# Two blocks of the first layer: plain first contractions, and second ones together by seven products of halves

## The chip, the cores and the metric

The kernel runs on one core of one Trainium2 chip. TensorE (PE in the profile) multiplies matrices, VectorE (DVE) and ScalarE (ACT) work elementwise, GpSimd (POOL) does a few small copies, and SyncE (SP) issues most DMAs. The metric is device time in microseconds (us): 1556.63 as the median of three runs (1556.58 to 1556.65).

## The reference

Linear attention without a softmax, an RMS norm per head, and two MLPs on the 4608 resulting tokens of width 512 (d_ff is 2048):

```python
kv = np.einsum('bhsd,bhse->bhde', k, v)        # q, k, v: (8, 8, 576, 64)
out = np.einsum('bhsd,bhde->bhse', q, kv)
rms = np.sqrt(np.mean(out * out, axis=-1, keepdims=True) + 1e-06)
x = (out / rms * g_norm)                       # then to (4608, 512)
# layer 1
h = x @ w_in                                   # 512 -> 2048
g = np.where(h >= 1, h, np.where(h <= -1, 0.0, (h + 1) ** 2 / 4))
x = g @ w_out                                  # 2048 -> 512
# layer 2
r = np.maximum(x @ w_in2, 0.0); out = (r * r) @ w_out2
```

Everything is float32.

## The kernel before

**Precision.** A float32 operand is split into a high part (a cast, L216) and a low part (the rest, a DVE subtraction, L229), and a product is three matmuls: high by high, high by low, low by high (`mm3`, L237; `mm_group` prints as L877). All counts of matmuls below contain this factor of three; one matmul is 128 x 128 weights against 512 columns.

**Blocks.** The tokens are cut into nine blocks of 512: block b (0 to 7) is the first 512 tokens of batch b, block 8 the eight remainders of 64. Layer 1 runs first over blocks 0 to 6 in the *plain* way: per block 16 steps f, each with 12 matmuls of the first contraction into a PSUM bank (`h_stage`, names `ph1_b_f`), the activation (relu on ACT L704, square on ACT L223, minimum and maximum on DVE L706), the split (`g_stage`: cast L216, rest L229), and, LAG = 2 steps later, 12 matmuls of the second contraction into four accumulators (`out_stage`, names `acc1_b_c`). `ph` has two PSUM buffers, the accumulators four banks.

Layer 1's blocks 7 and 8 and all pairs of layer 2 (`PAIRS`) are done two blocks at a time by *seven products of halves* instead of eight: `in_phase` forms sums of quarters of x, multiplies (336 matmuls, names `ph`), and combines on DVE; the activation follows; `out_phase` does the same with g (336 matmuls, names `po`). The sums of weight quarters are prepared earlier (`prep_load`, `prep_narrow`, `prep_sums`, `prep_split`), stored to DRAM, and loaded when wanted (`load_w2`, 512 KB each, on SP). A plain pair of blocks has 768 matmuls, a pair by seven products 672. The last block of layer 2 runs through the same phases with half the columns.

**Attention beside it.** While the plain blocks run, the attention of the next batches is worked in between. A batch has four *items*, one for each two heads (`hp`). An item is kv (`kv_stage`, once for two items), the transposes and splits of q (`t_stage`), q times kv (`o_stage`), and the norm (`r_stage`): row sums of squares on PE (`pr`, L600), Ln and Exp on ACT (L601, L603), a square on ACT (L223), then on DVE a Newton step for the two column halves (L518) and two products (L521, L522), at last the split of x (cast L216 on ACT, rest L229 on DVE). Its result `x1_b_hp` is the input of block b.

**What sets the order.** `hook(s, f)` puts a job into half-step s (two to a plain step, 32 to a block); before, item j of batch b starts at half-step 32(b - 1) + 7j, and its norm is six half-steps later. The sums of weights are spread from half-step 36 on over 164. Each engine executes its instructions in program order and waits there for what they need. `Ring` hands out tiles of SBUF again after their last use.

Of the kernel before, what the change touches and what calls it, by code (L numbers as in the profile page):

```python
# [76 lines left out]
def linear_attention_rms_two_mlps(  # L77
# [42 lines left out]
    xp = ctx.enter_context(tc.tile_pool(name="xp", bufs=2 * KD))  # L120
# [11 lines left out]
    PLAIN = B - 1  # L132
    PAIRS = [(2, 0), (2, 2), (1, PLAIN), (2, 4), (2, 6)]
# [332 lines left out]
    def kv_stage(b, *hps):  # L466
        ps = bank(b, f"pkv_{b}_{hps[0]}")
        for n, hp in enumerate(hps):
# [10 lines left out]
        for n, hp in enumerate(hps):  # L479
# [149 lines left out]

    def begin(b):  # L630
        if b < LAST_B:
            new_x(1, b)
# [17 lines left out]
    def attention(b, base, every, order):  # L650

        slots = []
        for j, hp in enumerate(order):
            s = base + every * j
            turn.setdefault((b, hp), len(turn))
            if b == 1:
                slots += [(max(0, s - 7), load_kv, b, hp), (s, kv_stage, b, hp)]
            elif j % 2 == 0:
                two = order[j : j + 2]
                turn[b, two[1]] = len(turn)  # L660
                slots += [(max(0, s - 7), load_kv, b, i) for i in two]
                slots.append((s, kv_stage, b, *two))
# [6 lines left out]
            if j == 0:  # L669
# [4 lines left out]
        if b < LAST_B:  # L674
            slots.append((2 * NF * b, store_xrem, b))
# [10 lines left out]
    def h_stage(L, b, f):  # L686
        pool, tag = (ps_h, "h")
        if (L, b) == (1, 0) and 2 <= f < WAVE:
            pool, tag = (ps_a, f"acc{f - 2}")
# [11 lines left out]
        u = ep.tile([P, TB], F32, tag="e", name=f"u{L}_{b}_{f}")  # L701
# [8 lines left out]
        gs[L, b, f] = u  # L710
# [70 lines left out]
    for L in [L for L, _ in PAIRS] + [2]:  # L781
        w_order += [(L, 0, q, p) for q in range(NQ) for p in PRODUCTS]
# [108 lines left out]
    def in_phase(n):  # L891
# [244 lines left out]
    for i, t in enumerate((7, 9, 11, 13, 15, 21, 23)):  # L1136
        hook(last + t, load_w2)
# [53 lines left out]
    for t in range(N1):  # L1191
        h_stage(*step(t))
# [15 lines left out]
        pay()  # L1208
# [79 lines left out]
```

## Time and profile before

| | us |
|---|---|
| median of three runs | 1556.63 |
| span of the profiled execution | 1555.3 |
| around that span (their difference) | 1.3 |
| PE busy | 1546.2 |
| DVE busy | 1133.4 |
| ACT busy | 973.7 |

The span runs from the first to the last instruction of one profiled execution; a run's time has about 1.3 us more. PE is busy 99% of the span. Matmuls are pipelined, so the time that one costs is not its own duration but the distance to the next; the chain of waits shows it, as us for so many matmuls.

### The profile page before, as it was taken

To read this page: it belongs to the slowest core of one execution; us is meant where nothing else is said; L and a number is where in the kernel's file an instruction comes from. 1 tells how busy PE (TensorE), PEld (TensorE's weight loads), DVE (VectorE), ACT (ScalarE), POOL (GpSimd) and SP (SyncE) were. 2 spreads that over 40 slices of the span, in tenths; PEclk is the share of its full clock that TensorE was granted. 3 is DMA by queue.
4 is the path that set the end of the run, shared out by engine and by line. 5 is a ranking of instruction groups with operands and counts; after the bars stand their busy time and mean duration, and the time that the engine had idled before them with its cause. 6 is when DMAs were issued, how large, how long until landed. Compare 5 with 4: busy or idle time off the path is not lost.

```text
span 1555.3 us, 22355 instructions
## 1 busy us (share of the span) xinstructions
PE 1546.2 (99%) x7729; PEld 1283.6 (83%) x7729; DVE 1133.4 (73%) x2000; ACT 973.7 (63%) x1833; POOL 20.4 (1%) x38
## 2 busy tenths in 40 slices
PE   9999999999999999999999999999999999999999
PEld 5787888888888888888888888888888888888898
DVE  6986886877877776754587558778965596568666
ACT  5977766767666676665565466456646663565374
POOL 0000000000000000000000000000000000000000
PEclk9999999999999999999999999999999999999999
DMA  9666899996878967935676877696876676877796
GB/s 290 194 217 187 274 315 277 309 314 196 275 246 243 281 207 228 295 99 169 196 245 192 224 219 245 194 250 191 258 228 204 203 239 197 242 248 223 214 389 250
DMA packets 327520, 368.23 MB, mean 237 GB/s; under 512 B 196976, under 2 KB 222576, under 8 KB 327408
## 3 DMA queue, kind: packets, MB, share of 16 engines
q1 hardware_dynamic: 295360, 308.60, 66.9%
q10 hardware_dynamic: 32048, 58.20, 9.9%
q8 instruction: 61, 1.00, 0.3%
q14 instruction: 51, 0.42, 0.1%
HBM read 282.59 MB, written 84.15 MB: 236 GB/s over the span
## 4 chain that ended last, share of the span: by engine, by line
PE 97%; ACT 1%; DVE 1%; DMA 1%; issue 0%; DVEq 0%; ACTq 0%
PE po L877 27%; PE ph L877 27%; PE acc L237 19%; PE ph L237 18%; PE po L237 1%; PE pkv L478 1%; PE pr L600 1%; PE pwarm L1150 1%; DMA wf<-wsd 1%; ACT raw L267 0%; ACT w L216 0%; PE pr L533 0%; ACT u L704 0%; DVE t L518 0%; DVE w L184 0%; PE po L510 0%
## 5 line engine op out<-in xcount | busy, mean ns | idle before, releaser
L877 PE MATMUL ph<-x,ws 128*128 128x512 f32 (+1 forms) x2016 | 422.4, 371 | 0.0
L877 PEld LDWEIGHTS ph<-x,ws 128*128 128x128 f32 x2016 | 355.9, 188 | 65.5
L877 PE MATMUL po<-t,ws 128*128 128x512 f32 x1680 | 381.6, 389 | 0.0
L877 PEld LDWEIGHTS po<-t,ws 128*128 128x128 f32 x1680 | 315.4, 188 | 65.4
L237 PE MATMUL ph<-x,w 128*128 128x512 f32 x1344 | 329.3, 392 | 1.3 <-ACT w L216 0.6
L237 PEld LDWEIGHTS ph<-x,w 128*128 128x128 f32 x1344 | 248.8, 188 | 54.0 <-ACT w L216 1.4
L806 DVE TENSOR_TENSOR t<-g,t 128x512 fp32r<-128x512 f32 (+1 forms) x288 | 183.2, 641 | 91.2 <-ACT t L216 84.2
L216 ACT CAST t<-g 128x512 fp32r<-128x512 f32 (+1 forms) x288 | 165.7, 585 | 97.2 <-DVE t L806 50.4
L237 PE MATMUL acc<-gs,w 128*128 128x512 f32 x696 | 173.0, 392 | 1.5 <-DVE u L706 1.5
L237 PE MATMUL acc<-gs,wt 128*128 128x512 f32 x648 | 157.9, 391 | 0.0
L237 PEld LDWEIGHTS acc<-gs,w 128*128 128x128 f32 x696 | 128.6, 188 | 27.8 <-DVE u L706 2.0
L934 DVE TENSOR_TENSOR h<-ph,e 128x512 f32<-128x512 f32 (+1 forms) x144 | 92.7, 645 | 67.4 <-PE ph L877 59.9
L237 PEld LDWEIGHTS acc<-gs,wt 128*128 128x128 f32 x648 | 120.1, 188 | 24.3
L704 ACT ACTIVATE u<-ph,halfb 128x512 f32<-128x512 f32 x112 | 77.3, 690 | 88.7 <-PE ph L237 86.3
L706 DVE SCALAR_TENSOR_TENSOR u<-u,ph 128x512 f32<-128x512 f32 x112 | 76.3, 681 | 54.2 <-ACT u L223 53.8
L941 ACT ACTIVATE h<-h 128x512 f32<-128x512 f32 (+1 forms) x120 | 70.3, 586 | 61.8 <-DVE h L934 57.1
L927 DVE TENSOR_TENSOR e<-ph,e 128x512 f32<-128x512 f32 (+1 forms) x96 | 60.9, 643 | 48.4 <-PE ph L877 47.4
L216 ACT CAST gs<-u 128x512 fp32r<-128x512 f32 x112 | 69.7, 622 | 38.4 <-DVE u L706 35.8
L229 DVE TENSOR_TENSOR gs<-u,gs 128x512 fp32r<-128x512 f32 x112 | 76.8, 686 | 21.7 <-ACT gs L216 21.2
L216 ACT CAST x<-xr 128x512 fp32r<-128x512 f32 (+1 forms) x84 | 49.0, 586 | 40.5 <-DVE xr L857 19.4
L942 ACT ACTIVATE g<-h 128x512 f32<-128x512 f32 (+1 forms) x120 | 70.7, 589 | 3.2
L223 ACT ACTIVATE u<-u 128x512 f32<-128x512 f32 x112 | 70.8, 632 | 1.5 <-ACT u L704 0.6
(134 smaller groups left out, 1531.8 us busy)
## 6 DMA issues: line engine op xcount, KB each, us to landing
ws<-wsd SPq DMA_DIRECT2D x336, 512.0 KB, 4.4
wsd<-s ACTq DMA_DIRECT2D x96, 512.0 KB, 4.9
wt<-wsd SPq DMA_DIRECT2D x54, 512.0 KB, 5.6
raw<-in_moe_w_in_dram SPq DMA_DIRECT2D x32, 512.0 KB, 6.0
raw<-in_moe_w_out_dram SPq DMA_DIRECT2D x32, 512.0 KB, 6.4
xr<-x1d SPq DMA_DIRECT2D x36, 256.0 KB, 4.9
out_dram<-ov SPq DMA_DIRECT2D x142, 64.0 KB, 3.7
wsd<-w SPq DMA_DIRECT2D x17, 512.0 KB, 5.0
```

The source lines that it names most:

```text
L216: return e.copy(dst, src)
L223: e.activation(dst, src, AF.Square)
L229: lo = engine(op + "_lo", phase).tensor_tensor(t[:, 1, :], src, t[:, 0, :].bitcast(F32), ALU.subtract)
L237: nc.tensor.matmul(dst, wt(a), xt(c), start=first and n == 0, stop=last and n == 2)
L704: nc.scalar.activation(u, ps, AF.Relu, bias=halfb, scale=0.5)
L706: nc.vector.scalar_tensor_tensor(u, u, 1.0, ps, op0=ALU.min, op1=ALU.max)
L806: engine2(op + "_lo").tensor_tensor(t[:, 1, :], src, t[:, 0, :].bitcast(F32), ALU.subtract)
L877: nc.tensor.matmul(ps, wt(a), xt(c), start=first and n == 0 and i == 0, stop=last and n == len(lhs) - 1 and i == 2, skip_group_check=True,)
L927: nc.vector.tensor_tensor(e[i, p], bank, e[i, 1], ALU.add)
L934: nc.vector.tensor_tensor(h, bank, add, ALU.add)
L941: nc.scalar.activation(u, h, AF.Relu)
L942: nc.scalar.activation(g, u, AF.Square)
```

## The change

PLAIN goes from 7 to 5 and PAIRS gains (1, 5). Blocks 5 and 6 of layer 1 run 16 plain steps each for the first contraction only, without `out_stage` between them (half-steps from FULL = 160 on are then one step of 12 matmuls each; the banks of the accumulators serve as further buffers of `ph`). The activation writes into tiles that stay whole (`whole_g`), and there is no `g_stage`. `whole_sums` (two DVE subtractions for each of eight k) forms the first sums in the last eight steps, and then `out_phase(0)` does the second contraction of both blocks by seven products. `in_phase(0)`, which was interleaved with the end of the plain part, is gone; the jobs that prepare x for the next pair move into `out_phase(0)`.

Attention from block 2 on starts at the half-steps STARTS, mostly 6 instead of 7 apart, with batch 7's items laid between those of batches 4 to 6 and after them; the sums of weights are spread over 149 half-steps instead of 164. Rings and tags of SBUF tiles change accordingly.

```diff
-    PLAIN = B - 1
-    PAIRS = [(2, 0), (2, 2), (1, PLAIN), (2, 4), (2, 6)]
+    PLAIN = 5
+    PAIRS = [(1, PLAIN), (2, 0), (2, 2), (1, B - 1), (2, 4), (2, 6)]
...
+    STARTS = (32, 39, 46, 53, 60, 66, 72, 78, 84, 90, 96, 102, 109, 115, 121, 127, 133, 140)
+    STARTS += (146, 152, 158, 164, 169, 175)
+    SPREAD = 149
...
     def h_stage(L, b, f):
...
+        if (b > PLAIN or (b == PLAIN and f >= 4)) and f % 3 < 2:
+            pool, tag = (ps_a, f"acc{f % 3 + f // 3 % 2 * 2}")
...
-        u = ep.tile([P, TB], F32, tag="e", name=f"u{L}_{b}_{f}")
+        if b >= PLAIN:
+            u = whole_g(f % NH, b - PLAIN)[:, f // NH, :]
+        else:
+            u = ep.tile([P, TB], F32, tag="e", name=f"u{L}_{b}_{f}")
...
+    def whole_g(k, m):
+        tiles = g_whole.setdefault(k, [])
+        if len(tiles) == m:
+            tiles.append(whole_ring.tile([P, 2, TB], F32, f"g0_{k}_{m}"))
+        return tiles[m]
...
+    whole_ring = Ring(
+        *((wp, f"w1_{i}") for i in range(10)),
+        *((xp, f"x{KD + i}") for i in range(KD)),
+        *((wp, f"w0_{i}") for i in range(2)),
+    )
...
+    def sums_in(n, k):
+        a, b, d = g2[k][0][:, 0, :], g2[k][0][:, 1, :], g2[k][1][:, 1, :]
+        t1[k] = t1_ring.tile([P, TB], F32, f"t1_{n}_{k}")[:, : width(n)]
+        engine2("t_sum").tensor_tensor(t1[k], b, a, ALU.subtract)
+        engine2("t_sum").tensor_tensor(b, d, b, ALU.subtract)
+
+    def whole_sums(k):
+        g2[k] = [Quarters(g_whole[k], j) for j in range(2)]
+        sums_in(0, k)
...
-    blocks = [(1, b) for b in range(PLAIN)]
+    blocks = [(1, b) for b in range(PLAIN + 2)]
+    FULL = 2 * NF * PLAIN
...
-        hooks.setdefault((s // 2, s % 2), []).append((f, a))
+        place = (s // 2, s % 2) if s < FULL else (PLAIN * NF + s - FULL, 0)
+        hooks.setdefault(place, []).append((f, a))
...
-    for b in range(1, B):
-        jobs += attention(b, 2 * NF * (b - 1), 7, range(NP))
+    jobs += attention((0, 7, 14, 21), [(1, hp) for hp in range(NP)])
+    order = []
+    for b in range(2, LAST_B):
+        order += [(LAST_B, b - 4)] * (b >= 4) + [(b, hp) for hp in range(NP)]
+    order.append((LAST_B, NP - 1))
+    jobs += attention(STARTS, order)
...
-        which, i = j % 2, j // 2
-        s0 = 2 * NF + 4 + (j * 164) // 16
+        which, i = 1 - j % 2, j // 2
+        s0 = 2 * NF + 4 + (j * SPREAD) // 16
...
-    last = 2 * (PLAIN - 1) * NF
-    first_x = x2_jobs(0, Ring(*[(st, "st")] * 7))
-    when = [2, 3, 3, 4, 5, 6, 7, 8, 7, 9, 9, 10, 11, 12, 13, 14]
-    for t, f in zip(when, first_x):
-        hook(last + 2 * t + 1, f)
+    for i in range(NH):
+        hook(FULL + NF + NH + i, whole_sums, i)
...
     for t in range(N1):
+        plain = t < PLAIN * NF
         h_stage(*step(t))
...
-        if not WAVE // 2 <= t < WAVE:
+        if plain and not WAVE // 2 <= t < WAVE:
             g_stage(*step(t))
-        if t >= WAVE:
+        if WAVE <= t < PLAIN * NF + LAG:
             out_stage(*step(t - LAG))
...
     for n in range(NS + 1):
-        step_in = in_phase(n)
+        step_in = in_phase(n) if n else ()
         for i, _ in enumerate(step_in):
             pay(True)
-            if n == 0 and i < LAG:
-                out_stage(*step(N1 - LAG + i))
```

**PE, start of block 6.** Names: `ph1_6_f` is the first contraction of block 6, `x1_6_c` its input (c = 3 is the last item of batch 6), `pr_6_3` the row sums of that item's norm, in two halves; `x3` stands for three matmuls. Before:

```order
L237 MATMUL acc1_5_0_5628<-gs1_5_13_6310,wt5_13_6283 128x512 x3
L237 MATMUL acc1_5_1_5629<-gs1_5_13_6310,wt5_13_6283 128x512 x3
L237 MATMUL acc1_5_2_5630<-gs1_5_13_6310,wt5_13_6283 128x512 x3
L237 MATMUL acc1_5_3_5631<-gs1_5_13_6310,wt5_13_6283 128x512 x3
L237 MATMUL ph1_6_0_6434<-x1_6_0_5665,w1_0_0_300 128x512 x3
L237 MATMUL ph1_6_0_6434<-x1_6_1_5666,w1_0_0_300 128x512 x3
L237 MATMUL ph1_6_0_6434<-x1_6_2_5667,w1_0_0_300 128x512 x3
L237 MATMUL ph1_6_0_6434<-x1_6_3_5668,w1_0_0_300 128x512 x3
L478 MATMUL pkv_7_0_6452<-v_7_0_6269,k_7_0_6266 64x64 x8
```

After (the same place in the work):

```order
L603 MATMUL pr_6_3_1_6376<-s2lo_6_3_6329,ones_121 128x288
L240 MATMUL ph1_6_1_6427<-x1_6_0_5748,w1_0_1_366 128x512
L240 MATMUL ph1_6_1_6427<-x1_6_1_5749,w1_0_1_366 128x512 x3
L240 MATMUL ph1_6_1_6427<-x1_6_2_5750,w1_0_1_366 128x512 x3
L240 MATMUL ph1_6_4_6518<-x1_6_2_5750,w1_0_4_487 128x512 x2
L240 MATMUL ph1_6_5_6538<-x1_6_0_5748,w1_0_5_508 128x512 x3
L240 MATMUL ph1_6_5_6538<-x1_6_1_5749,w1_0_5_508 128x512 x3
L240 MATMUL ph1_6_5_6538<-x1_6_2_5750,w1_0_5_508 128x512
L240 MATMUL ph1_6_3_6482<-x1_6_0_5748,w1_0_3_464 128x512 x3
L240 MATMUL ph1_6_3_6482<-x1_6_1_5749,w1_0_3_464 128x512 x3
L240 MATMUL ph1_6_3_6482<-x1_6_2_5750,w1_0_3_464 128x512 x3
L240 MATMUL ph1_6_5_6538<-x1_6_2_5750,w1_0_5_508 128x512 x2
```

The next five rows are products with `x1_6_3`. In the changed kernel the norm of the last item of batch 6 ends with the first row, and the products of `x1_6_0` to `x1_6_2` are drawn ahead of those of `x1_6_3`; before, all of x1_6 was there, and products of block 5's second contraction stood ahead.

**PE, end of the plain part.** `t0_p_k` are the operands of `out_phase(0)` in product p, `ws` sums of weights. Before:

```order
L237 MATMUL ph1_6_15_7338<-x1_6_3_5668,w1_0_15_1150 128x512 x3
L237 MATMUL acc1_6_0_6619<-gs1_6_13_7262,wt6_13_7239 128x512 x3
L237 MATMUL acc1_6_1_6620<-gs1_6_13_7262,wt6_13_7239 128x512 x3
L237 MATMUL acc1_6_2_6621<-gs1_6_13_7262,wt6_13_7239 128x512 x3
L237 MATMUL acc1_6_3_6622<-gs1_6_13_7262,wt6_13_7239 128x512 x3
L877 MATMUL ph0_1_0_7372<-x2_0_1_0_6731,ws2_0_0_1_6739 128x512 x3
L877 MATMUL ph0_1_0_7372<-x2_0_1_1_7076,ws2_0_0_1_6739 128x512 x3
L877 MATMUL ph0_1_1_7383<-x2_0_1_0_6731,ws2_0_0_1_6739 128x512 x3
L877 MATMUL ph0_1_1_7383<-x2_0_1_1_7076,ws2_0_0_1_6739 128x512 x3
```

After:

```order
L240 MATMUL ph1_6_15_6778<-x1_6_0_5748,w1_0_15_1150 128x512 x3
L240 MATMUL ph1_6_15_6778<-x1_6_1_5749,w1_0_15_1150 128x512 x3
L240 MATMUL ph1_6_15_6778<-x1_6_2_5750,w1_0_15_1150 128x512 x3
L240 MATMUL ph1_6_15_6778<-x1_6_3_5751,w1_0_15_1150 128x512 x3
L914 MATMUL po0_1_0_6817<-t0_1_0_6805,ws1_1_0_1_6576 128x512
L914 MATMUL po0_1_1_6818<-t0_1_0_6805,ws1_1_0_1_6576 128x512
L914 MATMUL po0_1_0_6817<-t0_1_0_6805,ws1_1_0_1_6576 128x512 x2
L914 MATMUL po0_1_1_6818<-t0_1_0_6805,ws1_1_0_1_6576 128x512 x2
L914 MATMUL po0_1_0_6817<-t0_1_1_6808,ws1_1_0_1_6576 128x512
L914 MATMUL po0_1_1_6818<-t0_1_1_6808,ws1_1_0_1_6576 128x512
```

Before, products of `in_phase` alternate with the second contraction of the last steps. In the changed kernel the first product of `out_phase(0)` stands right behind the last first contraction.

**DVE, the same place.** `g0_k_m` are the whole activations, L715 their minimum and maximum, L988 and L987 the sums, L843 the low part of an operand. After:

```order
L715 SCALAR_TENSOR_TENSOR g0_5_1_6551<-g0_5_1_6551,ph1_6_13_6736 128x512
L715 SCALAR_TENSOR_TENSOR g0_6_1_6592<-g0_6_1_6592,ph1_6_14_6757 128x512
L988 TENSOR_TENSOR g0_5_1_6551<-g0_5_1_6551 128x512
L988 TENSOR_TENSOR g0_6_1_6592<-g0_6_1_6592 128x512
L715 SCALAR_TENSOR_TENSOR g0_7_1_6613<-g0_7_1_6613,ph1_6_15_6778 128x512
L843 TENSOR_TENSOR t0_1_0_6805<-g0_0_0_5844,t0_1_0_6805 128x512
L988 TENSOR_TENSOR g0_7_1_6613<-g0_7_1_6613 128x512
L843 TENSOR_TENSOR t0_1_1_6808<-g0_1_0_5883,t0_1_1_6808 128x512
```

The low part of `t0_1_0`, which the first product of `out_phase(0)` needs, stands behind the last activation's minimum and maximum, which in the kernel before was followed by that activation's own split.

**DVE, ahead of the minimum and maximum of step 8 of block 2.** `t_b_hp` is the norm's value (L518 and L521 to L525), `s..` sums of weights. Before:

```order
L229 TENSOR_TENSOR gs1_2_7_2985<-u1_2_7_2937,gs1_2_7_2985 128x512
L270 SCALAR_TENSOR_TENSOR d2_0_10_3025<-raw2_0_10_2760,d2_0_10_3025 128x512
L229 TENSOR_TENSOR x1_3_1_2684<-t_3_1_2910,x1_3_1_2684 128x512
L491 TENSOR_TENSOR kvbd0_129<-pkv_3_2_2941,kvbd0_129 64x64
L557 STREAM_TRANSPOSE qf_3_2_2972<-q_3_2_2750 128x576
L491 TENSOR_TENSOR kvbd1_130<-pkv_3_2_2941,kvbd1_130 64x64
L360 TENSOR_TENSOR s12_2_0_2_3054<-d2_0_10_3025 128x256
L706 SCALAR_TENSOR_TENSOR u1_2_8_3020<-u1_2_8_3020,ph1_2_8_3007 128x512
```

After:

```order
L715 SCALAR_TENSOR_TENSOR u1_2_7_3036<-u1_2_7_3036,ph1_2_7_3023 128x512
L187 TENSOR_TENSOR s2_1_2_1_3067<-d2_1_10_2972,s2_1_2_1_3067 128x2x256
L232 TENSOR_TENSOR gs1_2_7_3070<-u1_2_7_3036,gs1_2_7_3070 128x512
L521 SCALAR_TENSOR_TENSOR t_3_2_3049<-pr_3_2_0_3040,t_3_2_3049 128x288
L521 SCALAR_TENSOR_TENSOR t_3_2_3049<-pr_3_2_1_3044,t_3_2_3049 128x288
L187 TENSOR_TENSOR s2_1_2_2_3087<-s12_2_1_2_3014,s2_1_2_2_3087 128x2x256
L524 SCALAR_TENSOR_TENSOR t_3_2_3049<-t_3_2_3049,wk0_3_2_2858 128x576
L364 TENSOR_TENSOR s34_1_1_2_3194<-j_1_2_3167 128x256
L525 TENSOR_TENSOR t_3_2_3049<-wk1_3_2_2859,t_3_2_3049 128x576
L187 TENSOR_TENSOR s2_1_2_3_3108<-s34_2_1_2_3015,s2_1_2_3_3108 128x2x256
L715 SCALAR_TENSOR_TENSOR u1_2_8_3104<-u1_2_8_3104,ph1_2_8_3091 128x512
L232 TENSOR_TENSOR x1_3_2_2615<-t_3_2_3049,x1_3_2_2615 128x512
```

In the changed kernel the four rows of the norm of item (3, 2) (two L521, L524, L525) and three of sums of weights stand between the minimum and maximum of steps 7 and 8. Before, the norm of item (3, 1) had ended here, and the kv rows and the transpose of item (3, 2) stood in this stretch.

## Rows read from the trace of the kernel before

**Rows 1.** The page's parts 1 and 4: busy time; chain by engine and line
```profile
span 1555.3 us, 22355 instructions
PE 1546.2 (99%) x7729; PEld 1283.6 (83%) x7729; DVE 1133.4 (73%) x2000; ACT 973.7 (63%) x1833; POOL 20.4 (1%) x38
...
PE 97%; ACT 1%; DVE 1%; DMA 1%; issue 0%; DVEq 0%; ACTq 0%
```

**Rows 2.** Busy us by stretch: PE, PEld, DVE, ACT, POOL, granted clock, DMA share, GB/s
```profile
50.00:60.00 10.00, 8.46 (x35) 6.10 (x36) 9.10 (x16) 9.75 (x20) 0.00 (x0) 1.00 1.01 299
...
150.00:240.00 90.00, 89.67 (x474) 74.16 (x474) 72.88 (x139) 64.26 (x127) 2.81 (x4) 1.00 0.92 288
...
420.00:510.00 90.00, 90.00 (x462) 75.07 (x458) 68.48 (x129) 62.34 (x126) 2.11 (x4) 1.00 0.80 249
...
786.00:862.00 76.00, 76.00 (x337) 62.94 (x336) 64.13 (x104) 41.26 (x72) 0.00 (x0) 1.00 0.72 221
```

**Rows 3.** Chain of waits at the plain part's end: start us, us, what
```profile
701.24 2.72 PE acc L237 x12
...
714.84 70.72 PE ph L877 x312
785.56 76.16 PE po L877 x336
```

**Rows 4.** Page's part 6, DMA issues: count, KB each, us to landing
```profile
ws<-wsd SPq DMA_DIRECT2D x336, 512.0 KB, 4.4
```

**Rows 5.** Timeline of one item's norm: start us, us, instruction [idle before <-releaser]
```profile
597.02 0.30 PE L600 MATMUL pr<-s2lo,ones 128*128 128x288 f32 x1
...
597.70 0.49 ACT L601 ACTIVATE wk<-pr,lnb 128x288 f32<-128x288 f32 x1
...
598.23 0.78 ACT L603 ACTIVATE wk<-wk,expb 128x576 f32<-128x576 f32 x1
...
600.12 0.69 ACT L704 ACTIVATE u<-ph,halfb 128x512 f32<-128x512 f32 x1 [1.12 <-PE ph L237]
600.70 0.68 ACT L223 ACTIVATE t<-wk 128x576 f32<-128x576 f32 x1
...
601.41 0.82 DVE L518 SCALAR_TENSOR_TENSOR t<-pr,t 128x288 f32<-128x288 f32 x2 [2.66 <-ACT t L223]
...
602.75 0.75 DVE L521 SCALAR_TENSOR_TENSOR t<-t,wk 128x576 f32<-128x576 f32 x1
...
604.02 0.75 DVE L522 TENSOR_TENSOR t<-wk,t 128x576 f32<-128x576 f32 x1
...
604.80 0.62 ACT L216 CAST x<-t 128x512 fp32r<-128x512 f32 x1 [0.80 <-DVE t L522]
...
605.67 0.68 DVE L229 TENSOR_TENSOR x<-t,x 128x512 fp32r<-128x512 f32 x1
```

**Rows 6.** Chain of waits around 50 us, with the distances of queued instructions
```profile
50.37 0.51 ACT u L223
50.88 0.52 ACT w L216
...
52.71 0.60 DVE d L270
```

**Rows 7.** Timeline, TensorE alone, the same place: its longest wait
```profile
53.96 0.96 PE L237 MATMUL acc<-gs,w 128*128 128x512 f32 x3 [1.54 <-DVE u L706]
```

**Rows 8.** Timeline, last step of block 6: activation and split
```profile
701.28 0.69 ACT L704 ACTIVATE u<-ph,halfb 128x512 f32<-128x512 f32 x1 [2.21 <-PE ph L237]
702.00 0.63 ACT L223 ACTIVATE u<-u 128x512 f32<-128x512 f32 x1
702.67 0.69 DVE L706 SCALAR_TENSOR_TENSOR u<-u,ph 128x512 f32<-128x512 f32 x1 [2.88 <-ACT u L223]
...
704.04 0.69 DVE L229 TENSOR_TENSOR gs<-u,gs 128x512 fp32r<-128x512 f32 x1 [0.69 <-ACT gs L216]
```

**Rows 9.** Chain of waits, the kernel's opening matmuls
```profile
1.19 4.88 PE pwarm L1150 x11
```

More of the change, by code (lines that the diff above doesn't have):

```diff
@@ L464, in load_first, with kv_stage @@
                     )
-    def kv_stage(b, *hps):
-        ps = bank(b, f"pkv_{b}_{hps[0]}")
-        for n, hp in enumerate(hps):
+    def kv_stage(*pairs):
+        ps = bank(pairs[0][0], "pkv_{}_{}".format(*pairs[0]))
+        for n, (b, hp) in enumerate(pairs):
             kt, vt = kvm.pop((b, hp))
@@ L478, in kv_stage @@
                     nc.tensor.matmul(ps[s, d], lhs, rhs, start=c == 0, stop=c == MR)
-        for n, hp in enumerate(hps):
+        for n, (b, hp) in enumerate(pairs):
             for j in range(2):
@@ L648, in attention_first, with attention @@
         return slots
-    def attention(b, base, every, order):
+    def attention(starts, order):
         slots = []
-        for j, hp in enumerate(order):
-            s = base + every * j
+        for j, (s, (b, hp)) in enumerate(zip(starts, order)):
             turn.setdefault((b, hp), len(turn))
             if b == 1:
-                slots += [(max(0, s - 7), load_kv, b, hp), (s, kv_stage, b, hp)]
+                slots += [(max(0, s - 7), load_kv, b, hp), (s, kv_stage, (b, hp))]
             elif j % 2 == 0:
                 two = order[j : j + 2]
-                turn[b, two[1]] = len(turn)
-                slots += [(max(0, s - 7), load_kv, b, i) for i in two]
-                slots.append((s, kv_stage, b, *two))
+                turn[two[1]] = len(turn)
+                slots += [(max(0, s - 7), load_kv, *i) for i in two]
+                slots.append((s, kv_stage, *two))
             slots += [
@@ L668, in attention @@
             ]
-            if j == 0:
+            if hp == 0 and b < LAST_B:
                 slots.append((s + 6, begin, b))
@@ L673, in attention @@
                 slots.append((s + 8, keep_x, b, hp))
-        if b < LAST_B:
-            slots.append((2 * NF * b, store_xrem, b))
+            elif hp == NP - 1:
+                slots.append((max(2 * NF * b, 0) if b < PLAIN + 1 else s + 9, store_xrem, b))
         return slots
@@ L709, in h_stage, with __init__, __getitem__ @@
             nc.vector.scalar_tensor_tensor(u, ps, 0.0, u, op0=ALU.max, op1=ALU.mult)
-        gs[L, b, f] = u
+        if b < PLAIN:
+            gs[L, b, f] = u
+    class Quarters:
+        def __init__(self, tiles, j):
+            self.tiles, self.j = tiles, j
+        def __getitem__(self, key):
+            p, m, s = key
+            return self.tiles[m][p, self.j, s]
+    def whole_g(k, m):
[3 more added lines that the diff above has]
+        return tiles[m]
     def g_stage(L, b, f):
@@ L768, in tile @@
             return pool.tile(shape, dtype, tag=tag, name=name)
-    w_ring = Ring(*((wp, f"w1_{i}") for i in (0, 1, 2, 3, 4, 13, 14, 15)))
-    t_ring = Ring(*[(gp, "g")] * 3, (wp, f"w0_{NF - 2}"), (wp, f"w0_{NF - 1}"))
-    g_ring = Ring(*[(xp, "x")] * 8, *((wp, f"w1_{5 + i}") for i in range(8)))
+    g_whole = {}
+    whole_ring = Ring(
[3 more added lines that the diff above has]
+    )
+    w_ring = Ring(
+        *((wp, f"w1_{i}") for i in (10, 11, 12, 13)), *((xp, f"x{i}") for i in range(KD))
+    )
+    t_ring = Ring(*[(gp, "g")] * 3, (wp, "w1_14"), (wp, "w1_15"))
+    g_ring = Ring(
+        *((xp, f"x{i}") for i in (4, 5, 6, 7, 0, 1, 2, 3)),
+        *((wp, f"w1_{i}") for i in (8, 9, 5, 6, 7, 10, 11, 12)),
+    )
     e_ring = Ring(*((ap1, t) for t in ("wk0", "wk1", "wk2", "hl0", "hl1")), (ap2, "q"))
@@ L780, in linear_attention_rms_two_mlps @@
     w_order = []
-    for L in [L for L, _ in PAIRS] + [2]:
-        w_order += [(L, 0, q, p) for q in range(NQ) for p in PRODUCTS]
+    for n, L in enumerate([L for L, _ in PAIRS] + [2]):
+        if n:
+            w_order += [(L, 0, q, p) for q in range(NQ) for p in PRODUCTS]
         w_order += [(L, 1, a, p) for p in PRODUCTS for a in range(NQ)]
@@ L1129, in linear_attention_rms_two_mlps @@
             hook(s0 + d, f, L, which, i, *a)
-    last = 2 * (PLAIN - 1) * NF
-    first_x = x2_jobs(0, Ring(*[(st, "st")] * 7))
-    when = [2, 3, 3, 4, 5, 6, 7, 8, 7, 9, 9, 10, 11, 12, 13, 14]
-    for t, f in zip(when, first_x):
-        hook(last + 2 * t + 1, f)
-    for i, t in enumerate((7, 9, 11, 13, 15, 21, 23)):
-        hook(last + t, load_w2)
+    for i in range(NH):
+        hook(FULL + NF + NH + i, whole_sums, i)
+    for s in (181, 183, 189, 190):
+        hook(s, load_w2)
     nc.scalar.preload_act_table_set("natural_log_exp_and_others")
@@ L1207, in linear_attention_rms_two_mlps @@
                 out_stage(*step(i))
-        pay()
+        if plain:
+            pay()
+    for _ in range(KD):
+        load_w2()
     late = []
@@ L1234, in linear_attention_rms_two_mlps @@
             for _ in steps:
-                pass
+                pay(True)
+            if n == 0:
+                w_ring.slots = [(wp, t) for t in ("w1_14", "w1_15", "w0_0", "w0_1")]
+                w_ring.slots += [(wp, f"w1_{i}") for i in range(4)]
+                t_ring.slots = [(gp, "g")] * 3 + [(wp, f"w0_{NF - 2 + i}") for i in range(2)]
             late = [lambda n=n, h=h: put_out(n, h // 2, h % 2) for h in range(4)]
```

30 lines of the change are left out of this document (15 added, 15 removed).

## The prediction, as it was recorded before the result was known

> **What bounds the kernel now.** First the busy shares and the chain of waits of the page. TensorE is busy 1546.2 of 1555.3 us, and the chain that ended last lies on it for 97% [rows 1]. A busy share alone does not prove a bound, so the stretches are read next, for TensorE without a hole: it has 90.00 of 90.00 us at 420 to 510 us and 76.00 of 76.00 at 786 to 862, at a granted clock of 1.00 [rows 2]. The chain at the end of the plain part then gives the price of TensorE's work: 12 matmuls in 2.72 us, 312 in 70.72, 336 in 76.16, that is 0.2267 us for each, in the plain products and in the seven products alike [rows 3]. So this kernel's time is its matmuls, and a change is worth what it takes from their number, less what makes TensorE wait.
>
> The reader should also see how near the other two engines are. DVE is busy 72.88 of 90 us in the fullest plain stretch and 68.48 in a usual one, ACT 64.26 and 62.34 [rows 2]: about 0.76 and 0.69 of the time. Each executes in order, so a wait of TensorE can come from the order on DVE long before DVE is full.
>
> **What goes.** The program has 6085 matmuls of 512 columns before and 6037 after: the 32 second contractions of 12 (384) of blocks 5 and 6 go, and 336 of seven products come. 48 x 0.2267 = 10.9 us off TensorE [rows 3]. The attention's matmuls only move.
>
> **What comes or moves and is costed at nothing.** ACT has 24 casts more and DVE 66 operations more. The operations are 0.60 us apart when queued [rows 6], so DVE has about 40 us more on 1133.4 [rows 1], spread over the kernel's length; TensorE's work covers it where the order allows (the places below are those where it does not). DMA: the sums of weights gain 28 loads of 512 KB on SP's queue and the tails of w_out lose 18. Such a load lands after 4.4 us [rows 4], and the moved engines' share is 0.72 in the stretch of the existing second contraction by seven products [rows 2]; the ring has eight tiles, each for 12 matmuls or 2.72 us, so loads are wanted some 20 us after their issue. If that cover were gone, one late load would cost up to 4.4 us. The sums of weights are packed closer, 149 half-steps instead of 164: a tenth more of this work for DVE and ACT in the plain part, within the shares above. Attention items at 6 instead of 7 half-steps put the same load into less time: DVE's 0.76 becomes at most 0.76 x 7/6 = 0.89 if all its work scaled with the items, which it does not.
>
> **Place A: start of block 6.** Block 6 needs `x1_6_3`, whose norm now ends just ahead. From its last row-sum matmul TensorE has, by the order, 27 matmuls (1 + 3 + 3 + 2 + 3 + 3 + 1 + 3 + 3 + 3 + 2) that do not need it: 27 x 0.2267 = 6.1 us. The kernel before shows the chain behind such a matmul: it ends at 597.32, the high part of x at 605.42, 8.1 us later, and the low part at 606.35, 9.0 us later [rows 5]. In that trace ACT stood for 1.12 us waiting for TensorE ahead of the square. By the changed order the chain is: first Ln and a square ahead of the second Ln 0.85, Ln 0.49, Exp 0.78, a queued cast 0.52, square 0.68, Newton 0.82, a split 0.60, product 0.75, a weight's rest 0.60, product 0.75, cast 0.62 [rows 5, 6], together 7.5 us. The wait for the high part is then 1.4 us (2.0 with the chain as before), and the low part follows 0.9 later, of which 0.45 is covered by two matmuls: about 1.9 us in all. After that q times kv of item (7, 3) wants a transposed and split q, which on DVE stands behind a 576-wide transpose (0.75, as such a product), four half-width sums (0.41 each, as half of the Newton pair's 0.82) and three of full width (0.60): with its own 0.75 some 4.9 us, about 4.5 since queued ones lie closer than they last [rows 5, 6]. TensorE has 13 matmuls of 512 and two short ones till then, 3.2 us: 1.3 us more. A: 3.2 us. Bounds: 0, if the scheduler's hold of 27 matmuls is enough because ACT has nothing queued; 5, if both chains take their time as shown.
>
> **Place B: from plain to seven products.** Before, the last activations' split was covered: relu began at 701.28 and the low part ended at 704.73 [rows 8], while 12 first products of another phase ran, then the rest without a gap [rows 3]. Now the first product of `out_phase(0)` stands right behind the last first contraction, and its low part stands on DVE behind the last activation's minimum and maximum. From the last matmul: relu 0.60 to the next, cast 0.52, square 0.63, queued operation on DVE 0.60, low part 0.69, and four handovers of 0.03 = 3.15 us [rows 6, 8]; two matmuls (0.45) can run on the high part. B: 2.7 us; 2.2 if the cast is out of the way, 3.1 if the split takes its time as shown.
>
> **Place C: closer attention in the plain part.** In block 2 the minimum and maximum of step 8 now stands behind the norm of item (3, 2). `ph` has two buffers, so step 10's products wait for it. From the last row sum TensorE has 7 + 12 + 12 = 31 matmuls = 7.0 us until step 10. DVE from the Newton step on: 0.82 + 0.60 + 0.75 + 0.41 + 0.75 + 0.60 + 0.69 = 4.6 us [rows 5, 6, 8]. Ahead of it ACT's chain took 4.1 us in the row before [rows 5]; without its wait for TensorE, but with a square between the two Ln (0.51) and two queued casts (1.04), it is 0.51 + 0.49 + 0.78 + 1.04 + 0.68 = 3.5. That is 8.1 to 8.7 against 7.0: 1.1 to 1.7 us; I take 1.2, near the lower end, since queued operations lie closer than they last. Other items stand so that the eviction comes ahead of the norm, and I find no other wait. C: 1.2 us; 0 to 5.
>
> **Sum.** -10.9 + 3.2 + 2.7 + 1.2 = -3.8 us on the profiled execution, 1555.3 to 1551.5 in span; with the 1.3 us around it that the median has, 1552.8 us. A difference of this kernel can be told from 0.2% on, 3.1 us (below 1553.5, above 1559.7).
>
> **The clock.** All of this stands on a TensorE clock of 1.00. The longest wait in the running kernel, 1.54 us at 53.96, left it at 1.00 over that stretch [rows 2, 7]. New waits of 2 to 3 us are longer than what the trace shows. The opening matmuls of the kernel, after TensorE had done nothing, took 4.88 us for 11, 0.444 each against 0.2267 [rows 9], about what 1.2 GHz instead of 2.4 would make of them, though the page's clock reads 1.00 there. The Trainium skill's page "TensorE: Matmul & The Clock Gate" (section "Why this matters for your kernels") says to avoid gaps between matmul bursts in mid-kernel, since idleness sends the clock back to its lower level; this case's trace has no wait after which that is seen. By the page the time would be that of the third rival.
>
> **Rivals.**
> - *All is hidden.* The waits at A, B and C are an artefact of counting hops: TensorE loses nothing and the whole 10.9 us comes: 1545.7 us. For it: after 60 us TensorE as good as never waits, though the order of before has similar pieces. Against it: the chain in rows 5 is longer than the cover at A, and B has no cover at all.
> - *The closer attention presses everywhere.* If C is not one place but the rule, a 1.2 us wait at half of the 21 items that start before half-step 160, ten of them, costs 12 us: -10.9 + 3.2 + 2.7 + 12 = +7, 1563.6 us. It decides the sign from about six such items on. For it: DVE at 0.81 in the fullest stretch [rows 2], with a tenth to come. Against it: at the present spacing not one item makes TensorE wait, and the order puts most evictions ahead of the norm.
> - *The clock falls.* After the waits of A and B TensorE runs for a time at its lower level. By rows 9 eleven matmuls then cost 11 x (0.444 - 0.2267) = 2.4 us, and four waits (two at A, one each at B and C) 9.6 us: 1562.4 us. For it: the opening. Against it: 1.54 us without effect.
>
> **Chances.** Forecast 0.71 (own range 1549.0 to 1556.5), all hidden 0.14, pressed attention 0.10, clock 0.05. The range to 8 in 10 takes the forecast's bounds (-10.9 + 2.2 = -8.7 to -10.9 + 5 + 3.1 + 5 = +2.2) and part of both sides: 1547.0 to 1559.5. Faster by over 0.2%: 0.41 of the forecast's 0.71, and all of the hidden case, 0.55. Within 0.2%: 0.29 of the forecast and a little of the two slow rivals, 0.32. Slower: the rest, 0.13.
>
> **What would show it.** In the changed kernel's trace: 12 matmuls in 2.72 us everywhere; 48 matmuls fewer; TensorE waiting once or twice some 6 us behind the last `pr` of item (6, 3), for x and then for qT (A), 2 to 3 us ahead of the first `po` matmul of the first pair (B), once in block 2 for a bank that DVE frees (C), and nowhere else after 60 us. Waits at many attention items, or a clock below 1.00 behind A and B, would make the prediction wrong, and so would a load of weight sums as the releaser.

## The result: 1573.55 us, slower by 1.1%

Over four runs the changed kernel took 1573.55 us (1572.31 to 1576.32), the kernel before over four 1556.64 (1556.58 to 1558.38): a ratio of 1.0108, 95% interval 1.0094 to 1.0123. Forecast were 1552.8 us and a range of 1547.0 to 1559.5. The sign was wrong, and the range too.

### The profile after

The page of the changed kernel, parts 1 and 4, beside [rows 1]:

```profile
span 1572.7 us, 22396 instructions
PE 1547.0 (98%) x7681; PEld 1277.8 (81%) x7681; DVE 1173.1 (75%) x2062; ACT 987.4 (63%) x1857; POOL 16.2 (1%) x38
...
PE 65%; DVE 2%; ACT 1%; DMA 1%; issue 1%; ACTq 0%; DVEq 0%
```

The chain of the changed kernel could be followed back only to 471.5 us, so its 65% on TensorE cannot be set beside the 97% of before. Line numbers of the changed kernel are a few higher than before (L240 is `mm3`, L715 the minimum and maximum).

48 records of TensorE are gone as forecast (7729 to 7681), yet its busy time has not fallen by 10.9 us: it is 0.8 us longer. Matmuls at a lower clock count as busy for longer (below). The price where nothing waits has stayed, as the chain behind the plain part shows:

```profile
803.07 76.16 PE po L914 x336
```

The span is 17.4 us longer, so 17.4 + 10.9 = 28.3 us of new loss have come in. TensorE's waits between 240 and 660 us (us in all, times, longest) say where it begins:

```profile
PE po L240 <- DVE qT L562: 6.0, 1, 6.0
PE ph L240 <- ACT x L219: 3.8, 1, 3.8
PE ph L240 <- DVE u L715: 1.8, 2, 1.5
PE po L914 <- ACT t L219: 1.3, 1, 1.3
PE po L914 <- DVE t L843: 1.1, 1, 1.1
PE acc L240 <- ACT ev L768: 1.1, 1, 1.1
```

The third is place C (forecast 1.2 us), the fourth and fifth place B (forecast 2.7, measured 1.28 + 1.12 = 2.4), the second place A (forecast 3.2). The largest one was not in the prediction. Its timeline, all engines:

```profile
401.55 1.51 SPq L318 DMA_DIRECT2D wf<-wsd  x1
...
402.26 0.76 DVE L560 STREAM_TRANSPOSE qf<-q 128x576 f32<-128x576 f32 x1
...
402.95 0.38 DVE L272 TENSOR_SCALAR d<-raw 128x512 int32<-128x512 int32 x1
...
405.39 0.42 PE L240 MATMUL po<-qT,kvbd 128*128 128x288 f32 x2
...
409.95 0.69 DVE L343 TENSOR_TENSOR wf<-wf 128x512 f32<-128x512 f32 x1 [6.62 <-DMA wf<-wsd]
410.67 0.42 DVE L363 TENSOR_TENSOR s<-j,wf 128x256 f32<-128x256 f32 x1
411.02 0.75 DVE L562 TENSOR_TENSOR qT<-qf,qT 128x576 fp32r<-128x576 f32 x1
...
411.82 1.33 PE L240 MATMUL po<-qT,kvbd 128*128 128x288 f32 x4 [6.01 <-DVE qT L562]
...
412.94 2.77 PE L240 MATMUL ph<-x,w 128*128 128x512 f32 x6
...
415.50 0.45 PE L603 MATMUL pr<-s,ones 128*128 128x288 f32 x1
...
418.18 0.39 PE L240 MATMUL acc<-gs,wt 128*128 128x512 f32 x1
```

`wf` is a tile of w_out's tail (its rows f = 7 to 15 don't stay in SBUF), loaded again so that the sums of weights can be formed (`prep_load`, `prep_join`). It was issued at 401.55 and landed some 8.4 us later; DVE stood in front of the join for 6.62 us, and the transposed q of an attention item, which TensorE wanted from 405.5 on, stood close behind it. The nine loads of wf landed after (shortest, median, longest):

```profile
DMA to landing us min/median/max: 3.9/5.5/9.4
```

In the kernel before it was 4.5, 5.3 and 7.8. DVE waits for such loads in both kernels:

```profile
DVE wf L340 <- DMA wf<-wsd: 19.4, 7, 4.5
```

is the kernel before (over the whole span), and

```profile
DVE wf L343 <- DMA wf<-wsd: 15.0, 6, 6.6
```

the changed one. The total is no larger; what has gone is the cover.

The second part of the loss stands behind the waits. Busy time by stretch, columns as in [rows 2]:

```profile
270.00:300.00 30.00, 28.46 (x132) 23.25 (x131) 23.97 (x44) 22.33 (x46) 0.64 (x1) 1.00 0.97 289
405.00:420.00 15.00, 8.99 (x32) 7.37 (x31) 6.14 (x11) 5.14 (x13) 0.00 (x0) 0.66 0.56 171
610.00:620.00 10.00, 9.76 (x33) 7.55 (x34) 7.74 (x15) 6.86 (x15) 0.24 (x1) 0.70 0.65 221
640.00:660.00 20.00, 17.59 (x70) 13.73 (x69) 17.93 (x31) 12.50 (x22) 0.00 (x0) 0.91 0.75 256
```

The granted clock is below 1.00 in the three stretches with the waits of 6.01, 3.85 and 1.28 + 1.12 us, and 1.00 where the wait was 1.54. From 412.94 six matmuls take 2.56 us until the next one at 415.50, 0.43 each, where six cost 1.36 before [rows 3]: the lower of the two levels, 1.2 instead of 2.4 GHz. What that costs is read from TensorE's timeline at places C, A and B:

```profile
285.54 1.43 PE L240 MATMUL ph<-x,w 128*128 128x512 f32 x5 [1.54 <-DVE u L715]
...
600.09 6.31 PE L240 MATMUL ph<-x,w 128*128 128x512 f32 x27
610.24 5.40 PE L240 MATMUL ph<-x,w 128*128 128x512 f32 x11 [3.85 <-ACT x L219]
615.44 0.44 PE L240 MATMUL po<-qT,kvbd 128*128 128x288 f32 x1
...
647.42 0.73 PE L914 MATMUL po<-t,ws 128*128 128x512 f32 x2 [1.28 <-ACT t L219]
649.27 13.03 PE L914 MATMUL po<-t,ws 128*128 128x512 f32 x49 [1.12 <-DVE t L843]
```

Eleven matmuls from 610.24 to 615.44 are 5.20 us against 2.49: 2.7 lost. From 411.82 to 418.18, behind the twelfth `ph` matmul, it is 6.36 against 3.4: 3.0 lost. Behind B 49 matmuls last 13.03 us against 11.30 in e10 below: 1.7 lost. So the three places cost 9.0, 6.6 and 4.1 us; with C's 1.5 and two waits of 1.1 and 0.7 around 462 and 467 (the first behind an accumulator's eviction on ACT that stood 3.6 us for a store) that is 23 of the 28.3 us. The rest lies in smaller pieces.

### The profile page after: what moved, and what is told of

Read it like the earlier page. It is cut to its first block, busy times and chain, and to the rows that moved or that the text cites. A ratio compares the mean times of both kernels' runs of the same rounds, so it can differ in the third digit from the quotient of the medians.

```text
span 1572.7 us, 22396 instructions
## 1 busy us (share of the span) xinstructions
PE 1547.0 (98%) x7681; PEld 1277.8 (81%) x7681; DVE 1173.1 (75%) x2062; ACT 987.4 (63%) x1857; POOL 16.2 (1%) x38
## 4 chain that ended last, share of the span: by engine, by line
PE 65%; DVE 2%; ACT 1%; DMA 1%; issue 1%; ACTq 0%; DVEq 0%
PE po L914 32%; PE ph L914 27%; PE ph L240 5%; DMA wf<-wsd 1%; PE acc L240 1%; DVE s L187 0%; DVE wf L343 0%; PE pr L603 0%; PE pkv L481 0%; PE po L240 0%; DVE g L715 0%; DVE t L521 0%; ACT s L219 0%; DVE s2lo L589 0%; DVE d L273 0%
## 5 line engine op out<-in xcount | busy, mean ns | idle before, releaser
L914 PE MATMUL po<-t,ws 128*128 128x512 f32 x2016 | 460.0, 390 | 2.4 <-ACT t L219 1.3
L914 PEld LDWEIGHTS po<-t,ws 128*128 128x128 f32 x2016 | 379.4, 188 | 82.2 <-ACT t L219 1.7
L240 PE MATMUL ph<-x,w 128*128 128x512 f32 x1344 | 338.8, 397 | 6.9 <-ACT x L219 3.8
L240 PEld LDWEIGHTS ph<-x,w 128*128 128x128 f32 x1344 | 250.5, 190 | 62.1 <-ACT x L219 4.3
L843 DVE TENSOR_TENSOR t<-g,t 128x512 fp32r<-128x512 f32 (+1 forms) x336 | 215.8, 648 | 92.8 <-ACT t L219 90.9
L219 ACT CAST t<-g 128x512 fp32r<-128x512 f32 (+1 forms) x336 | 196.7, 590 | 129.6 <-PE po L914 71.6
L240 PE MATMUL acc<-gs,w 128*128 128x512 f32 x528 | 134.9, 394 | 3.0 <-DVE u L715 1.5
L240 PEld LDWEIGHTS acc<-gs,w 128*128 128x128 f32 x528 | 97.2, 188 | 23.7 <-DVE u L715 2.0
L240 PE MATMUL acc<-gs,wt 128*128 128x512 f32 x432 | 108.0, 392 | 0.0
L240 PEld LDWEIGHTS acc<-gs,wt 128*128 128x128 f32 x432 | 79.5, 188 | 15.8
L715 DVE SCALAR_TENSOR_TENSOR u<-u,ph 128x512 f32<-128x512 f32 x80 | 54.4, 680 | 21.9 <-ACT u L226 21.6
L713 ACT ACTIVATE u<-ph,halfb 128x512 f32<-128x512 f32 x80 | 55.6, 695 | 17.4 <-PE ph L240 15.2
L978 ACT ACTIVATE u<-ph 128x512 f32<-128x512 f32 (+1 forms) x40 | 22.1, 552 | 62.6 <-PE ph L914 61.8
```

What stands on the lines that cost most here:

```text
L219: return e.copy(dst, src)
L240: nc.tensor.matmul(dst, wt(a), xt(c), start=first and n == 0, stop=last and n == 2)
L713: nc.scalar.activation(u, ps, AF.Relu, bias=halfb, scale=0.5)
L715: nc.vector.scalar_tensor_tensor(u, u, 1.0, ps, op0=ALU.min, op1=ALU.max)
L843: engine2(op + "_lo").tensor_tensor(t[:, 1, :], src, t[:, 0, :].bitcast(F32), ALU.subtract)
L914: nc.tensor.matmul(ps, wt(a), xt(c), start=first and n == 0 and i == 0, stop=last and n == len(lhs) - 1 and i == 2, skip_group_check=True,)
```

## The experiments

Each run is set beside the kernel before in the same rounds (medians 1556.8 to 1557.3), and the interval is that of the ratio to it. Differences to the changed kernel (1573.55) are across rounds.

**Without the late loads.**

```diff
-                if which == 1 and f >= NF - TAIL:
+                if False:
...
-                w = (wi[L, f] if which == 0 else wo[L, f]).bitcast(F32)
+                w = (wi[L, f] if which == 0 else wo[L, f % (NF - TAIL)]).bitcast(F32)
```

> The changed kernel, but the sums of the second half of w_out's rows are made from tiles that lie in SBUF, so the nine wf loads (and nothing else) go; the sums are of other weights than they should be. Late-load theory: TensorE's waits of 6.2 us at 405.5 and most of the 4.0 us at 606, with the slow stretches behind them (3.0 us each), come from DVE standing in front of a wf load; they go, and so do about 1 us at 476 and 537: 9 to 16 us faster, 1558 to 1564 us. Dense-attention rival: DVE is full and the wait shows up at another item; at most 4 us faster, 1569 us or more.

1559.8 us, 1.0020 (1.0010 to 1.0029): 13.8 us faster than the changed kernel. The wait at 405 is gone, as is place A's 3.85. The same edit in the kernel before:

> The kernel before with the same nine loads left out (sums of other weights). DVE waited 19.4 us for them in its trace, TensorE never. Late-load theory: within 1 us of 1556.6, since the attention at 7 half-steps left slack. If the loads cost time by themselves, it is several us faster and the theory needs no dense attention.

1557.11 us, 0.9997 (0.9988 to 1.0006). The loads cost the kernel before no time that can be told.

**The loads kept, but early.** In the list of jobs for each pair of sums (first number: half-step):

```diff
+    LOAD1 = 2
...
+            (LOAD1, 1, prep_load, ()),
             (2, 2, prep_narrow, (0,)),
...
+            (5, 1, prep_join, ()),
...
-            (7, 1, prep_load, ()),
-            (9, 1, prep_join, ()),
```

and the join writes into another tile (`d_tile`) instead of into wf.

> The changed kernel with the same wf loads issued five half-steps earlier, ahead of the layer-2 sums in the ring of four tiles, and joined at once into another tile; everything is computed. Late-load theory: as without the loads, 9 to 16 us faster, 1558 to 1564 us. Dense-attention rival: at most 4 us faster. If only the DMA traffic of the loads mattered and not their lateness, no faster than the changed kernel.

1560.6 us, 1.0022 (1.0013 to 1.0031): nearly the whole effect with all loads in place, and DVE waits for none of the nine in its trace. It is their lateness and not their traffic. TensorE's timeline shows what place A is without them:

```profile
589.48 6.57 PE L240 MATMUL ph<-x,w 128*128 128x512 f32 x28
597.44 0.73 PE L240 MATMUL ph<-x,w 128*128 128x512 f32 x2 [1.40 <-ACT x L219]
598.64 2.34 PE L240 MATMUL ph<-x,w 128*128 128x512 f32 x9 [0.46 <-DVE x L232]
...
603.11 0.80 PE L240 MATMUL po<-qT,kvbd 128*128 128x288 f32 x4 [0.96 <-DVE qT L563]
```

1.40, 0.46 and 0.96 us: the prediction had 1.4, 0.5 and 1.3.

**The first operands early** (place B):

```diff
+        if t == N1 - 1:
+            first_jobs = x2_jobs(1, tmp)
+            first_at = (2, *range(10, 8 + 2 * len(first_jobs), 2))
+            first_out = out_phase(0, first_jobs, first_at)
+            next(first_out)
         h_stage(*step(t))
...
+        else:
+            steps = first_out
```

> The changed kernel, but the first operands t0_1_0 to t0_1_2 of the second contraction are split ahead of the last first contraction instead of behind it. Price of place B in the trace: 4.5 us of excess between TensorE's starts from 645.7 to 653.0, of which about 2.7 are two waits and the rest a slow clock. If that is right: 4 us faster, 1569.5 us. Rival: the splits push the last activations back on ACT and DVE, and the wait only moves: within 1 us of 1573.5.

1570.84 us, 2.7 us faster than the changed kernel, not 4. One wait of 1.3 us for the low part stayed: on DVE two sums of the whole tiles still stood ahead of it. The granted clock over 640 to 660 us is 1.00 again.

**Closer items alone.**

```diff
-        jobs += attention(b, 2 * NF * (b - 1), 7, range(NP))
+        jobs += attention(b, 2 * NF * (b - 1), 6, range(NP))
```

> The kernel before, with the items of each batch 6 half-steps apart instead of 7 and nothing else changed (blocks 5 and 6 plain, wf loads where they were). Late-load theory: DVE's 19.4 us of waits for wf, covered at 7, come through at some items: TensorE waits that it did not have, 2 to 8 us slower, 1559 to 1565 us. Rival (the loads are late only through the new order of the weight sums): no TensorE wait beyond those of before, within 1 us of 1557.

1567.09 us, 1.0065 (1.0050 to 1.0080), 10 us slower, beyond both ranges and not for the reason expected. Between 140 and 560 us TensorE is without a wait (420.00 of 420.00 busy), though DVE stood 18.8 us for wf. The loss is one wait at the end of the plain part with a lower clock behind it (0.77 over 650 to 665 us), and some 2 us at 108 to 116:

```profile
651.40 0.62 ACT L216 CAST x<-xr 128x512 fp32r<-128x512 f32 x1 [4.08 <-DMA xr<-x1d]
...
653.46 0.67 ACT L216 CAST qT<-qf 128x576 fp32r<-128x576 f32 x1 [0.93 <-DVE qf L557]
...
654.19 0.85 PE L237 MATMUL po<-qT,kvbd 128*128 128x288 f32 x2 [6.31 <-ACT qT L216]
```

Again an in-order engine stands in front of a load, here ACT for x of the next pair. My theory that closer items by themselves uncover the wf loads fell.

**Mending A and B.** e6 is e3 with `STARTS` ending in `(146, 152, 157, 162, 166, 174)`; e7 is e6 with e4's edit at `t == N1 - 4`.

> e3 (early wf load) and the last items of batch 6 moved up by one to three half-steps (STARTS ends 146, 152, 157, 162, 166, 174), so that x1_6_3 is there before block 6 begins. In e3's trace place A still costs 3.6 us (waits of 1.40, 0.46 and 0.96). If lateness of that item is the cause, 3 us faster than e3: 1557 to 1558 us. Rival: batch 6 pressed closer makes waits in block 5 instead, no faster than e3.

> e6 and the first operands of the second contraction split three steps ahead of the last first contraction. Sum of excess left by e3's trace beyond the kernel before: A 3.6, B 4.2, others about 5. With A and B gone: 10.9 us less work and 5 us of waits, 1551 us (1549 to 1554). If the order on DVE only hands the waits on, 1556 or more.

e6: 1558.47 us, 1.0008 (0.9999 to 1.0017), 2 us faster than e3; the wait left at place A is 0.67 us. e7: 1560.12 us, 1.0020 (1.0010 to 1.0029), a miss: with the operands early the third load of weight sums was late, and TensorE waited for it:

```profile
634.71 1.19 PE L915 MATMUL po<-t,ws 128*128 128x512 f32 x4 [0.48 <-DVE t L844]
638.97 1.32 PE L915 MATMUL po<-t,ws 128*128 128x512 f32 x3 [3.07 <-DMA ws<-wsd]
```

That load's tile had been one of the four through which the sums go. e10 turns their cycle by one tile, with e4's edit at `t == N1 - 3`; e11 adds wider items in batch 3:

```diff
-    prep_tags = itertools.cycle(range(NF - TAIL + RING + 2, NF))
+    prep_tags = itertools.cycle((NF - 1, NF - 4, NF - 3, NF - 2))
```

> e6, with the first operands of the second contraction split two steps ahead of the last first contraction, and the ring of four tiles of the sums begun one tile later, so that the tiles that the third and fourth load of weight sums take come free earlier. e6's trace has 4.2 us left at place B, e7's showed that operands alone hand the wait to that third load (3.1 us). With both gone: e6 less 4 us, 1554 to 1555 us. If the wait is handed on once more: 1557 or more.

> e10 with the items of batch 3 seven half-steps apart instead of six and those behind them moved by one to three, so that the norm of item (3, 2) is not queued ahead of the eviction of step 8 of block 2. Place C and its neighbour cost 1.7 us beyond the usual in e6's trace: 1.5 us faster than e10, 1552 to 1554 us. Rival: the later items meet the sums elsewhere, no faster than e10.

e10: 1554.01 us (1552.50 to 1555.15), 0.9980 (0.9971 to 0.9989): faster than the kernel before by 2.8 us. That is a part of the 10.9 us that the products save, and no run shows the whole. In the profiled execution the span is 4.2 us below that of before, so 6.7 us of new loss are left. TensorE's longest new waits are 1.0 and 0.9 us; between 140 and 560 us it is busy 417.49 us, before 419.67, and the rest of the loss is not taken apart. At B it no longer waits:

```profile
span 1551.1 us, 22399 instructions
...
PE 1538.9 (99%) x7679; PEld 1273.1 (82%) x7681; DVE 1171.0 (75%) x2062; ACT 986.7 (64%) x1857; POOL 15.7 (1%) x38
```

```profile
604.16 24.93 PE L240 MATMUL ph<-x,w 128*128 128x512 f32 x109
628.92 11.30 PE L915 MATMUL po<-t,ws 128*128 128x512 f32 x49
```

e11: 1560.34 us, 1.0026 (1.0016 to 1.0035). Place C went, but other items met other work: one wait of 2.6 us in the norm's row sums. The rival held.

**What took the cover away.** First the sums moved against the items, `s0` by three half-steps:

> The changed kernel with all work on the weight sums, wf loads included, three half-steps earlier against attention and matmuls; nothing else. Collision theory: DVE still stands some 15 us for the wf loads in all, but the instruction right behind the join is another one than the transposed q of an attention item, so the 6.2 us wait at 405 and the 3.0 us of slow clock behind it go or shrink: 1562 to 1569 us. Rival (at this density any late load comes through to TensorE): waits of the same sum at other places, 1571 to 1577 us.

> As e8, three half-steps later. Collision theory: the wait at 405 goes or shrinks here too, but the last sums fall later behind the start of block 6 and the first loads of out_phase: 1562 to 1575 us, with the sum of DVE's waits for wf about as before (15 us). Rival: 1571 to 1577 us.

1574.45 us, 1.0112 (1.0097 to 1.0127), and 1581.2 us, 1.0161 (1.0141 to 1.0181), the second above both its ranges. The wait at 405 is gone in both, and others of about the same sum stand elsewhere: TensorE's busy time of 140 to 560 us is 407.85 and 407.28 of 420, against 409.23 in the changed kernel. So it is not the collision of one pair of instructions. Then the order (`which, i = 1 - j % 2, j // 2`) and the spread (149 for 164) of the sums, put into the kernel before in steps:

> The kernel before with one thing changed: in each pair of weight sums W_out's come ahead of W_in's (items still 7 half-steps apart, sums over 164). Order theory: the wf loads then fall where they are not covered, DVE's waits for them rise above 19.4 us and TensorE waits: 5 to 15 us slower, 1562 to 1572. Rival (the order only matters together with closer items): within 2 us of 1557.

> As e14, and the sums over 149 half-steps instead of 164, as in the changed kernel; items still 7 apart. If order and spread are the cause whatever the items' distance: at least e14 plus some us, 1567 to 1585. Rival: within 2 us of 1557.

> The kernel before with items 6 half-steps apart (as e5) and also the weight sums as in the changed kernel: W_out first and spread over 149 half-steps. Blocks 5 and 6 stay as before, and between two batches there are still 8 half-steps without a new item. Order theory: the order of the sums takes the cover away; waits of several us between 150 and 560 us, 1570 to 1580 us. Rival (the unbroken row of items does): as e5, no wait beyond the usual there, 1565 to 1570 us.

Order alone, e14: 1558.38 us, 1.0009 (1.0000 to 1.0019), a miss; DVE stood 20.9 us for wf and TensorE did not wait. With the spread, e15: 1566.70, 1.0062 (1.0047 to 1.0077). With the items 6 apart as well, e12: 1594.44, 1.0234 (1.0216 to 1.0253), 14 us above the range of the order theory; DVE stood 35.7 us for wf. TensorE's busy time of the 420 us from 140 on, columns as in [rows 2], first e14, then e15, then e12:

```profile
140.00:560.00 420.00, 419.67 (x2184) 348.85 (x2183) 325.75 (x606) 291.88 (x580) 10.66 (x17) 1.00 0.87 268
```

```profile
140.00:560.00 420.00, 413.88 (x2138) 342.16 (x2137) 325.23 (x607) 284.11 (x569) 7.60 (x17) 1.00 0.87 273
```

```profile
140.00:560.00 420.00, 405.04 (x2077) 331.88 (x2076) 315.92 (x586) 273.25 (x550) 5.67 (x16) 0.98 0.83 264
```

In e15, with the old items and the old blocks, one wait of 5.35 us shows the mechanism by itself:

```profile
402.41 0.69 DVE L340 TENSOR_TENSOR wf<-wf 128x512 f32<-128x512 f32 x1 [7.70 <-DMA wf<-wsd]
...
404.08 0.68 DVE L706 SCALAR_TENSOR_TENSOR u<-u,ph 128x512 f32<-128x512 f32 x1
...
404.81 3.54 PE L237 MATMUL ph<-x,w 128*128 128x512 f32 x8 [5.35 <-DVE u L706]
```

Last, the changed kernel with W_in's sums first again, and without the items of batch 7 between the others:

> The changed kernel with W_in's sums ahead of W_out's again, as in the kernel before; sums over 149 half-steps, items as changed. Order theory: the 6.2 us wait at 405 and most of what follows go, 1560 to 1566 us (e1 without the loads: 1560); the last W_out sums are later, which may cost 1 to 3 us at the start of out_phase. Rival (any order at this density): 1571 us or more.

> The changed kernel without the two items of batch 7 that lie between batches 3, 4 and 5 (the results of the last two items stand in for them, so block 7 is not what it should be); the third one moves to the end. There are 12 half-steps between the items at 78 and 90 and at 109 and 121. The wf loads stay. Order theory: the 6.2 us wait at 405 stays, 1572 to 1576 us plus what the closer end costs. Rival (the unbroken row): with the pauses DVE catches up, the wait at 405 goes or falls under 2 us, 1562 to 1568 us.

e16: 1570.37 us, 1.0084 (1.0067 to 1.0101); the wait at 405 goes, many of about 1 us come, and those at place B grow from 2.4 to 5.7 us. e13: 1571.92 us, 1.0096 (1.0080 to 1.0112), not to be told from the changed kernel; DVE stood 21.9 us for wf and waits of up to 4.5 us remained. No single part is the cause: in the kernel before the order costs 1.5 us, the spread on top of it 8, the distance alone 10, and all three together 37. What is shown is that the lateness of these loads carries some 13 of the 17 us. Why a given load lands after 8 us instead of 5 was not tried by itself; SP waited 26.7 us in all ahead of wf loads for stores of earlier sums, but 20.9 in the kernel before too.

## Why the prediction was wrong, step by step

- *What goes*: right. 48 matmuls less, and where nothing waits, 336 in 76.16 us as before. That the kernel would keep these 10.9 us but for A, B and C was not right: e10 has next to no waits left at A and B, and keeps 2.8. That its 1554.0 lies near the forecast of 1552.8 is luck, since the forecast had 7.1 us of waits at A, B and C. (The 66 more operations of DVE are 62 in the trace.)
- *"The sums of weights are packed closer ... within the shares above", costed at nothing*: the step that failed. It asked whether DVE and ACT had room, and weighed lateness for `ws` alone. The page's chain for the kernel before lists "DMA wf<-wsd 1%", and its waits show DVE standing 19.4 us for wf; neither was read. It also took the median of 4.4 us for the most that one late load can cost, where the load at 401.55 landed after 8.4 us and held TensorE for 6.01. That W_out's sums now come ahead of W_in's has no term at all. With the lateness gone the kernel gains 13 us (e1, e3).
- *Place A*: the chain was right to 0.5 us without the loads (e3), 3.85 us and 2.7 us of slow clock with them.
- *Place B*: 2.4 us against 2.7, and 1.7 us of clock. *Place C*: 1.54 against 1.2.
- *The clock*, given 5%: it fell behind A, behind B and behind the wait at 405, which this rival did not have, and cost 7.4 us, where the rival had 9.6. A clock below 1.00 behind A and B was one of the prediction's own signs of being wrong. The page on the clock gate in the Trainium skill ("TensorE: Matmul & The Clock Gate", "Why this matters for your kernels") warned of gaps, and the trace agrees: 0.66 behind 6.01 us, 0.70 behind 3.85. I let the one wait of 1.54 us without effect speak against it, although I forecast longer ones.
- *The pressed attention*, given 10%, had sign and size (1563.6) nearer than the forecast, but another mechanism: not the eviction behind the norm at ten items, but a load ahead of DVE's queue. Waits for that eviction are 1.8 us in two places of the changed kernel; they lead in e9 (9.8 us in five places), e8 and e16 (4.7 each), where the sums had been moved.

## What to carry to other kernels

Where one engine is full, list the waits of the engines that are not, above all an in-order engine that stands in front of a DMA: such a wait can cost nothing while its neighbours in the queue are early (19.4 us here), and much once the schedule is packed closer (13 us of time for 15.0 us of waits). Ask of a packed schedule when each load is issued and what stands behind its consumer, not only whether the shares have room. And price a wait of the matmul engine with the slow matmuls behind it.

## What the runs showed of the hardware

A wait of TensorE of 6.01 or 3.85 us was followed by some 11 or 12 matmuls 0.43 to 0.47 us apart; waits of 1.54 us were not. Single waits of 3.07 us (e7) and 2.63 us (e11) were followed by a clock of 0.83 (over 635 to 645 and 395 to 405 us). Two waits of 1.28 and 1.12 us with only two matmuls between them also brought it down (0.91 over 640 to 660 us), a single one of 1.25 us at the same place in e4 did not. The changed kernel's four runs spread over 4.0 us, 25 runs of the kernel before (beside e1 to e4) over 3.0 (1556.18 to 1559.15); the granted clock of the changed one's executions lay between 0.993 and 0.996.
